# The memory update as one-head products on four column strips

## The chip, the cores and the metric

The kernel runs on one core of a Trainium2 chip. The metric is the device time of one execution in microseconds, the median over runs. Engines are named as in the profile: PE is TensorE (PEld its weight loads), DVE is VectorE, ACT is ScalarE, POOL is GpSimd, SP is SyncE, which issues most transfers.

## The reference

One normalised input goes through a segmented attention with a memory and through a gated unit; both are added to the input. There are 2048 tokens of width 448, 16 heads of 28, and 4 segments of 512 tokens. Cut to what matters here:

```python
phi = lambda t: jnp.where(t > 0, t + 1.0, jnp.exp(t))
for s in range(N):
    qs, ks, vs = q[:, :, s], k[:, :, s], v[:, :, s]
    logits = jnp.einsum("bhqd,bhkd->bhqk", qs, ks) * scale + mask
    p = _softmax(logits, axis=-1)
    a_dot = jnp.einsum("bhqk,bhkd->bhqd", p, vs)
    pq = phi(qs)
    num = jnp.einsum("bhld,bhde->bhle", pq, M)
    den = jnp.einsum("bhld,bhd->bhl", pq, z)[..., None] + 1e-6
    outs.append(g * (num / den) + (1.0 - g) * a_dot)
    pk = phi(ks)
    M = M + jnp.einsum("bhld,bhle->bhde", pk, vs)
    z = z + jnp.einsum("bhld->bhd", pk)
# with xn the layer norm of x:
return x + attention(xn) @ wo + ((sigmoid(xn @ w_gate) * (xn @ w_up)) @ w_down)
```

The change concerns the last two lines of the loop: `M` and `z`, the memory of each head.

## The kernel before, in words

The kernel has two parts. The front goes through the four segments, called blocks, `b` = 0 to 3. For each block it makes the values of four token tiles (`values`, L361), then keys and queries in seven chunks of 128 columns (`keys_queries`, L381), called the seven steps `k` below, and interleaves with them the normalising and transposing of the next block's tokens (`normalise`, `turn`, L103). Behind the front come the attention over keys and values (scores L639, sums L725), the gated unit (L255, L181) and the output product (L824), interleaved by a plan of ticks. TensorE, ScalarE and VectorE run each in the order in which the program issues for them; in the front the order of POOL and SP is left to the framework.

For blocks 0 to 2 the memory is updated in the front. `key_rows` (steps 2 to 5) transposes a chunk of phi of the keys (L401) and copies it to `kn`: tokens on partitions, four token tiles, 448 key columns. `vst` holds the values of the block: tokens on partitions, 16 heads of 32 columns, of which 28 are values and 4 are ones, so that a product with `kn` gives `M` and `z` at once. `update(b, i)` handles group `i` of four heads: four products, one for each token tile, of 112 key columns with 128 value columns. Their 112x128 result holds the wanted 28x32 blocks of the four heads on its diagonal and products of different heads beside it; `heads`, a mask of ones and zeros made once by POOL (L522 to L526), clears these. VectorE multiplies by it and adds the old memory (L412 in block 0, L415 and L416 later). The memory `mst` is two sets of four tiles of 112x128, so packed, that blocks use in turn. Updates of groups 0 and 1 stand in steps 4 and 5, those of groups 2 and 3 in step 6. Their banks of PSUM are "pd" and "m" in turn; there is one bank each.

The memory is read by `recall` (L427): one product of a 112x128 memory tile with phi of the queries (112x512), for group `i`. The recalls of block 1 stand in block 2, those of block 2 at the beginning of block 3, those of block 3 at its end. What they give is weighed and goes to DRAM by a transfer that POOL issues (L431).

In the attention, `Unit.finish` (L725) already uses the four column strips of TensorE's array: head `j` of a group writes partitions `32j` to `32j + 31` of one bank:

```python
for kb in range(NT):
    for j in range(HG):
        T.matmul(pa[32 * j:32 * j + 32, kb * P:], self.vv[:, kb, 32 * j:32 * j + 32],
                 self.pairs[j // 2].block(j % 2, kb), start=kb == 0, stop=kb == NT - 1)
```

Of the kernel before, what the change touches and what calls it, by code (L numbers as in the profile page):

```python
# [9 lines left out]
F32 = mybir.dt.float32  # L10
F32R = mybir.dt.float32r
AF = mybir.ActivationFunctionType
ALU = mybir.AluOpType
# [3 lines left out]
P = 128  # L17
D = 448
H = 16
DH = 28  # L20
# [3 lines left out]
NT = 4  # L24
F = 1792
NF = F // P
HG = 4
NG = H // HG
GW = HG * DH
# [40 lines left out]
def kernel(  # L70
# [10 lines left out]
    nc = tc.nc  # L81
    V, A, G, T = nc.vector, nc.scalar, nc.gpsimd, nc.tensor
# [33 lines left out]
    def x_block(b):  # L116
        return x[b * L:(b + 1) * L, :].rearrange("(t p) d -> p t d", p=P)
# [5 lines left out]
    def bank(name, tag):  # L123
        return ps.tile([P, L], F32, name=name, tag=tag, bufs=banks[tag])
# [5 lines left out]
    def pad(pool, nbytes):  # L130
        pool.tile([P, nbytes // 4], F32, name="pad", tag="pad", bufs=1)
# [3 lines left out]
    def weigh(pool, num, g, add):  # L135

        r = pool.tile([P, 16], F32, name="rc", bufs=2)
        n3 = num.rearrange("p (m c) -> p m c", c=32)
        if add:
            V.tensor_scalar_add(r, n3[:, :, DH], add)  # L140
            V.reciprocal(r, r)
        else:
            V.reciprocal(r, n3[:, :, DH])
        V.scalar_tensor_tensor(n3[:, :, :DH], n3[:, :, :DH], g, r.unsqueeze(2).to_broadcast([P, 16, DH]),
                               op0=ALU.mult, op1=ALU.mult)
# [8 lines left out]
    def eight_k(dtype, name):  # L154
        return mid.tile([P, 8, 256], dtype, name=name, tag="8k")
# [144 lines left out]


    with tc.tile_pool(name="front", bufs=2) as sb, tc.manual_schedule(engines=FRONT):
        heads = sb.tile([P, P], F32, name="heads", bufs=1)
        pad(sb, 192)
        stage = eight_k(F32, "stage").rearrange("p (c a) n -> p c (a n)", c=4)
        vst = eight_k(F32, "vst").rearrange("p (t a) (h c) -> p t (a h) c", t=NT, c=32)
        wv = [late_pair("wv") for _ in range(4)]
        wv = [wv[c // 2][:, c % 2, :] for c in range(8)]
        wqk = [sb.tile([P, 8, P], F32R, name=f"wqk{c}", bufs=1) for c in range(7)]
        mst = [[sb.tile([GW, P], F32, name=f"mst{n}_{i}", bufs=1) for i in range(NG)] for n in range(2)]  # L310
        one = sb.tile([P, 1], F32, name="one", bufs=1)
        kn = eight_k(F32, "kn").rearrange("p (t a) n -> p t (a n)", t=NT)

# [11 lines left out]
        def root(vh):  # L325
            y = sb.tile([P, vh.shape[1]], F32, name=f"y{vh.shape[1]}")
            A.activation(y, vh, AF.Sqrt, scale=-2.0)
            return y
# [40 lines left out]
        def values(b, t):  # L369
            pv = bank("pv", "p")  # L370
            value_terms(b, t, pv, EARLY[1] if b == 0 else TERMS)
            store_values(b, t, pv)
# [29 lines left out]
            n = min(P, D - c * P)  # L402
            A.activation(kn[:, :, c * P:c * P + n], pk.rearrange("p (t n) -> p t n", t=NT)[:, :, :n], AF.Copy)

        def update(b, i):

            pmm = bank("pmm", ("pd", "m")[i % 2])
            for t in range(NT):
                T.matmul(pmm[:GW, :P], kn[:, t, i * GW:(i + 1) * GW], vst[:, t, HG * i:HG * (i + 1), :],  # L409
                         start=t == 0, stop=t == NT - 1)  # L410
            if b == 0:
                V.tensor_mul(mst[1][i], pmm[:GW, :P], heads[:GW])  # L412
            else:
                dm = sb.tile([GW, P], F32, name="dm")
                V.tensor_mul(dm, pmm[:GW, :P], heads[:GW])  # L415
                V.tensor_add(mst[(b + 1) % 2][i], mst[b % 2][i], dm)  # L416

        def phi_queries(b, i):
            phi = sb.tile([GW, L], F32, name="phi", tag="e", bufs=5)
            nc.sync.dma_start(phi, fd[b][i * GW:(i + 1) * GW])  # L420
            return phi

        def recall(b, i, phi):
            ts = sb.tile([P, L], F32, name="ts", bufs=1)
            tb = sb.tile([P, L], F32, name="tb", bufs=2)
            n2 = bank("n2", ("m", "pd")[i % 2])
            T.matmul(n2, mst[b % 2][i], phi, start=True, stop=True)  # L427
            V.transpose(ts, n2)
            weigh(sb, ts, gate[:, i:i + 1], MEM_EPS)
            V.transpose(tb, ts)  # L430
            nc.gpsimd.dma_start(od[b][P * i:P * (i + 1)], tb)  # L431
# [28 lines left out]
        def split_qk(c):  # L460
            r = raw_qk[c].rearrange("p (c n) -> p c n", c=4)
            A.activation(wqk[c][:, 0:4, :], r, AF.Copy)
            G.tensor_sub(wqk[c][:, 4:8, :], r, wqk[c][:, 0:4, :].bitcast(F32))
# [18 lines left out]
        p3, xn, st, y = {}, {}, {}, {}  # L482
# [20 lines left out]
        for t in range(2):  # L503
# [15 lines left out]
        turn_low(3)  # L519
        split_qk(1)  # L520
        split_qk(2)
        G.memset(heads, 1.0)  # L522
        h3 = heads.rearrange("p (j c) -> p j c", c=32)
        G.affine_select(h3, h3, pattern=[[-DH, HG], [0, 32]], base=0, channel_multiplier=1,
                        compare_op=ALU.is_ge, fill=0.0)
        G.affine_select(h3, h3, pattern=[[DH, HG], [0, 32]], base=DH - 1, channel_multiplier=-1,  # L526
                        compare_op=ALU.is_ge, fill=0.0)

        ffn = gated()
        for b in range(NB):  # L530
            last = b == NB - 1
            phi, xn = {}, {}
            if b > 1:
                phi = {i: phi_queries(b - 1, i) for i in range(NG)}
            st = None
            for t in range(3 if b == 0 else 0, NT):
                values(b, t)
                if b > 1 and t > 0:
                    recall(b - 1, t - 1, phi[t - 1])
                if b == 0:  # L540
                    split_qk(t)
                if last:
                    continue
                if t == (3 if b == 0 else 0):
                    mv, vh = statistics(b + 1, 0, NT)
                if t == (3 if b == 0 else 0):
                    st = mv, vh, root(vh)
                if t == (3 if b == 0 else 2):
                    A.activation(one, ident[:, 0:1], AF.Exp)
            if st and b > 0:  # L550
                st = rstd(*st)
                for n in range(2):
                    xn[n] = normalise(b + 1, n, *st[n])
            e = {}
            for k, c in enumerate((3, 4, 5, 6, 0, 1, 2) if last else range(7)):
                e[c] = keys_queries(b, c)
                if b == 0 and c + 4 < 7:
                    split_qk(c + 4)
                if k == 0:
                    if b > 1:  # L560
                        recall(b - 1, NG - 1, phi[NG - 1])
                    if b == 0:
                        st = rstd(*st)
                    if b == 0:
                        A.activation(gate, gate, AF.Exp, scale=-1.0)
                        V.tensor_scalar_add(gate, gate, 1.0)
                        V.reciprocal(gate, gate)
                        V.tensor_scalar(gate_n, gate, -1.0, 1.0, op0=ALU.mult, op1=ALU.add)
                if (b, k) in ((0, 3), (1, 0)):
                    with tc.issue_after(stored[b, c]):  # L570
                        nc.sync.dma_start(acc[b + 2], x_block(b + 2))
                if (b, k) in ((2, 1), (3, 0)):
                    with tc.issue_after(stored[b, c]):
                        next(ffn)
                if last:
                    if k > 0:
                        next(ffn)
                    if 2 <= k < 6:
                        phi[k - 2] = phi_queries(b, k - 2)
                    if k > 4:  # L580
                        begin[k - 5]()
                        recall(b, k - 5, phi[k - 5])
                    continue
                if 2 <= k < 6:
                    key_rows(k - 2, e[k - 2])
                if 4 <= k:
                    update(b, k - 4)
                if k == 6:
                    update(b, 3)
                n = k - 1 if b == 0 else k + 1  # L590
                if 2 <= n < 6:
                    turn(b + 1, n - 2, xn[n - 2])
                if 0 <= n < 4 and n not in xn:
                    xn[n] = normalise(b + 1, n, *st[n])
                if b == 2 and k == 6:
                    next(ffn)
            if last:
                for i in range(2):
                    for _ in range(FILLS[i]):
                        next(ffn)  # L600
                    if i == 0:
                        begin[2]()
                    recall(b, i + 2, phi[i + 2])
# [3 lines left out]
    sb = ctx.enter_context(tc.tile_pool(name="att", bufs=1, reuse_waits="tile"))  # L607
# [234 lines left out]
    with tc.manual_schedule(engines=MANUAL):  # L842
        next(steps)
        k = sum(FILLS) + 6
# [46 lines left out]
```

## Time and profile before

| | |
|---|---|
| median of three runs | 685.7 us (685.55 to 686.2) |
| span of the profiled execution | 684.2 us |
| TensorE busy | 678.0 us (99%) |
| VectorE, ScalarE, POOL busy | 570.1, 338.5, 141.6 us |
| the memory products (L409) | 96 instructions, 34.4 to 115.0 us |
| the recalls (L427) | 24 instructions, 82.6 to 156.4 us |

The span runs from the first to the last instruction of the profiled execution; a time of its own for that execution is not listed, and the runs' times hold 1.5 us (at the median) that the span does not. Busy times are the union of an engine's instructions. A product's recorded duration runs to an estimated end and overlaps the next one's, so prices are read from starts, not from durations. In lines that list a group of instructions, the numbers behind `x` are the busy time of all and the mean of one in ns, and behind the last bar the idle time ahead of them and what ended it. Every f32 product is two instructions on TensorE.

### The profile page before, as it was taken

What the parts mean: (1) busy time and instruction counts of PE and PEld (TensorE: products, weight loads), DVE (VectorE), ACT (ScalarE), POOL (GpSimd) and SP (SyncE); (2) the same over time, 40 slices, a digit from 0 to 9 for tenths busy, and PEclk for the clock granted to TensorE, in tenths of its full rate; (3) what the DMA queues carried; (4) which work ended last, traced back from release to release, by engine and by line L of the source; (5) the groups of instructions that cost most, each with busy time, mean ns of one, the idle gap of its engine ahead of it and who ended that gap; (6) DMA issues with size and microseconds to landing.
All of it is one profiled execution on the core that took longest, in us unless ns stands there. A gap on an engine that the chain in (4) does not pass through costs nothing.

```text
span 684.2 us, 10501 instructions
## 1 busy us (share of the span) xinstructions
PE 678.0 (99%) x3594; PEld 566.7 (83%) x3594; DVE 570.1 (83%) x995; ACT 338.5 (49%) x563; POOL 141.6 (21%) x349
## 2 busy tenths in 40 slices
PE   8999999999999999999999999999999999999998
PEld 7898878778888888888888878788787887888897
DVE  6765696767799899999999899899998999899854
ACT  4836555343365445645456455455554555545320
POOL 3500010101212232232212213133121231221000
PEclk9999999999999999999999999999999999999999
DMA  8446656696223332252424343333353332523352
GB/s 268 173 159 224 214 195 256 234 336 194 71 67 97 104 90 68 57 150 54 108 57 101 91 110 69 100 57 99 84 94 94 97 69 68 115 63 92 86 165 104
DMA packets 45940, 84.37 MB, mean 123 GB/s; under 512 B 6336, under 2 KB 20544, under 8 KB 45376
## 3 DMA queue, kind: packets, MB, share of 16 engines
q1 hardware_dynamic: 42736, 76.26, 37.0%
q0 software_dynamic: 3008, 7.34, 5.2%
q8 instruction: 28, 0.46, 0.3%
q14 instruction: 24, 0.20, 0.1%
q10 hardware_dynamic: 144, 0.11, 0.0%
HBM read 51.05 MB, written 32.64 MB: 122 GB/s over the span
## 4 chain that ended last, share of the span: by engine, by line
PE 97%; DMA 1%; DVE 1%; SPq 0%; ACT 0%; issue 0%; DVEq 0%
PE pgu L255 41%; PE pd L181 20%; PE pp L381 10%; PE st L639 6%; PE pa L725 5%; PE po L824 5%; PE pv L361 5%; PE pmm L409 2%; PE n L427 2%; DMA acc<-in_x 1%; PE pt L103 1%; PE pk L401 1%; DVE stats L320 0%; DVE xs L110 0%; DVE xn L346 0%
## 5 line engine op out<-in xcount | busy, mean ns | idle before, releaser
L255 PE MATMUL pgu<-xs,wgu 128*128 128x512 f32 x1232 | 302.6, 393 | 0.0
L255 PEld LDWEIGHTS pgu<-xs,wgu 128*128 128x128 f32 x1232 | 228.9, 188 | 46.3 <-issue 2.0
L181 PE MATMUL pd<-wdn,hh 128*128 128x448 f32 x672 | 155.3, 366 | 0.0
L181 PEld LDWEIGHTS pd<-wdn,hh 128*128 128x128 f32 x672 | 122.7, 188 | 11.6 <-issue 0.8
L654 POOL TENSOR_SCALAR_AFFINE_SELECT w<-w 128x256 f32<-128x256 f32 (+1 forms) x160 | 76.0, 478 | 231.5 <-ACT w L643 162.4
L707 ACT ACTIVATE w<-w 128x1024 f32<-128x1024 f32 (+1 forms) x96 | 87.8, 915 | 57.6 <-DVE w L703 57.6
L643 ACT ACTIVATE w<-st 128x512 f32<-128x512 f32 x128 | 75.6, 592 | 61.4 <-PE st L639 58.5
L703 DVE TENSOR_TENSOR w<-w,mb 128x1024 f32<-128x1024 f32 (+1 forms) x96 | 100.5, 1054 | 0.8
L661 DVE TRANSPOSE_TENSOR_REDUCE mx<-w 128x32 f32<-128x1024 f32 x64 | 78.9, 1233 | 6.6 <-POOL w L654 6.5
L381 PE MATMUL pp<-xs,wqk 128*128 128x512 f32 x308 | 77.7, 401 | 0.0
L183 DVE TENSOR_TENSOR acc<-pd,acc 128x448 f32<-128x448 f32 x112 | 67.5, 602 | 5.6 <-PE pd L181 5.5
L278 ACT ACTIVATE hh<-sg 128x512 fp32r<-128x512 f32 x56 | 35.4, 631 | 67.9 <-DVE sg L272 46.0
L381 PEld LDWEIGHTS pp<-xs,wqk 128*128 128x128 f32 x308 | 56.8, 188 | 13.4 <-issue 2.4
L639 PE MATMUL st<-qk 84*128 84x128 f32 (+3 forms) x256 | 62.0, 313 | 0.0
L262 ACT ACTIVATE sg<-pgu 128x512 f32<-128x512 f32 x56 | 33.2, 592 | 50.8 <-PE pgu L255 48.9
L639 PEld LDWEIGHTS st<-qk 84*128 84x128 f32 x256 | 47.9, 189 | 8.7 <-issue 1.4
L272 DVE SCALAR_TENSOR_TENSOR sg<-sg,pgu 128x512 f32<-128x512 f32 x56 | 37.7, 673 | 11.2 <-PE pgu L255 11.2
L388 DVE TENSOR_TENSOR qk<-pp,qk 128x512 fp32r<-128x512 f32 x28 | 19.3, 688 | 29.8 <-ACT e L386 23.7
L689 DVE STREAM_TRANSPOSE mb<-top 128x1024 f32<-128x1024 f32 x32 | 39.5, 1235 | 3.3 <-POOL top L686 3.2
L361 PE MATMUL pv<-wv,xs 128*128 128x448 f32 x176 | 39.6, 376 | 0.4 <-DVE xs L110 0.3
L281 DVE SCALAR_TENSOR_TENSOR hh<-sg,hh 128x512 fp32r<-128x512 f32 x56 | 38.1, 680 | 0.9 <-ACT hh L278 0.9
L725 PE MATMUL pa<-w,vv 128*32 128x128 f32 (+3 forms) x512 | 37.8, 436 | 0.0
(100 smaller groups left out, 636.0 us busy)
## 6 DMA issues: line engine op xcount, KB each, us to landing
qk<-qd SPq DMA_DIRECT2D x192, 112.0 KB
qd<-qk SPq DMA_DIRECT2D x28, 512.0 KB
raw<-in_w_ffn SPq DMA_DIRECT2D x14, 512.0 KB
vd<-vst SPq DMA_DIRECT2D x4, 1024.0 KB
vv<-vd SPq DMA_DIRECT2D x16, 256.0 KB
od<-w POOLq DMA_DIRECT2D x16, 256.0 KB, 4.2
sums<-od SPq DMA_DIRECT2D x32, 128.0 KB
out<-acc SPq DMA_DIRECT2D x15, 224.0 KB
```

The source lines that it names most:

```text
L181: T.matmul(pd[:, :D], l, r, start=n == 0, stop=n == len(mms) - 1)
L183: V.tensor_add(acc[b][:, t, :], pd[:, :D], acc[b][:, t, :])
L255: T.matmul(dst, wgu[f][:, w, side * P:(side + 1) * P], xs[b][:, a, :], start=n == 0, stop=n == len(TERMS) - 1)
L361: T.matmul(pv[:, :D], xs[b][:, a, t * P:(t + 1) * P], wv[w], start=n == 0, stop=n == len(TERMS) - 1)
L381: T.matmul(pp, wqk[c][:, w, :], xs[b][:, a, :], start=n == 0, stop=n == len(TERMS) - 1)
L639: T.matmul(st[:, at:at + L - kb * P], self.qk[:KS, 1, h, kb * P:(kb + 1) * P], self.qk[:KS, 0, h, kb * P:], start=True, stop=True)
L643: A.activation(w, st, AF.Copy)
L654: G.affine_select(d, d, pattern=pattern, base=0, channel_multiplier=-1, compare_op=ALU.is_ge, fill=MASK)
L661: V.tensor_reduce(self.mx[:, 32 * h:32 * h + 32], w3[:, h, :2 * L].rearrange("p (b n) -> p b n", n=32), axis=mybir.AxisListType.X, op=ALU. ...
L703: V.tensor_sub(w, w, m)
L707: A.activation(w, w, AF.Exp, scale=SCALE)
L725: T.matmul(pa[32 * j:32 * j + 32, kb * P:], self.vv[:, kb, 32 * j:32 * j + 32], self.pairs[j // 2].block(j % 2, kb), start=kb == 0, stop=k ...
```

## The change

`update` is called once a block, in step 6, and does all four groups in bank "m". Every head has products of its own: 28 key columns with its 32 value columns, for each of four token tiles, head `j` of a group on strip `j`. The results lie dense: head `j` of group `i` on partitions `32j` to `32j + 27`, columns `32i` to `32i + 31`. VectorE copies (block 0) or adds the old sums (later) strip by strip, four instructions, into `dense`, and for each strip a transfer that POOL issues puts the new sums on the packed diagonal of `mst`, whose other parts POOL has set to zero once. The mask is gone, and so is `dm`. `recall` reads a group's slice of the one `mst` tile.

```diff
-        heads = sb.tile([P, P], F32, name="heads", bufs=1)
...
-        mst = [[sb.tile([GW, P], F32, name=f"mst{n}_{i}", bufs=1) for i in range(NG)] for n in range(2)]
+        mst = [sb.tile([GW, NG, HG, 32], F32, name=f"mst{n}", bufs=1) for n in range(2)]
+        dense = [sb.tile([P, NG, 32], F32, name=f"dense{n}", bufs=1) for n in range(2)]
...
-        def update(b, i):
-
-            pmm = bank("pmm", ("pd", "m")[i % 2])
-            for t in range(NT):
-                T.matmul(pmm[:GW, :P], kn[:, t, i * GW:(i + 1) * GW], vst[:, t, HG * i:HG * (i + 1), :],
-                         start=t == 0, stop=t == NT - 1)
-            if b == 0:
-                V.tensor_mul(mst[1][i], pmm[:GW, :P], heads[:GW])
-            else:
-                dm = sb.tile([GW, P], F32, name="dm")
-                V.tensor_mul(dm, pmm[:GW, :P], heads[:GW])
-                V.tensor_add(mst[(b + 1) % 2][i], mst[b % 2][i], dm)
+        def update(b):
+
+            pmm = bank("pmm", "m")
+            for i in range(NG):
+                for t in range(NT):
+                    for j in range(HG):
+                        h = HG * i + j
+                        T.matmul(pmm[32 * j:32 * j + DH, 32 * i:32 * i + 32], kn[:, t, DH * h:DH * (h + 1)],
+                                 vst[:, t, h, :], start=t == 0, stop=t == NT - 1)
+            p3 = pmm[:, :P].rearrange("p (i c) -> p i c", c=32)
+            new, old = dense[(b + 1) % 2], dense[b % 2]
+            for j in range(HG):
+                strip = slice(32 * j, 32 * j + DH)
+                if b == 0:
+                    V.tensor_copy(new[strip], p3[strip])
+                else:
+                    V.tensor_add(new[strip], p3[strip], old[strip])
+                nc.gpsimd.dma_start(mst[(b + 1) % 2][DH * j:DH * (j + 1), :, j, :], new[strip])
...
-            T.matmul(n2, mst[b % 2][i], phi, start=True, stop=True)
+            T.matmul(n2, mst[b % 2][:, i].rearrange("p j c -> p (j c)"), phi, start=True, stop=True)
...
-        G.memset(heads, 1.0)
...
+        for n in range(2):
+            G.memset(mst[n], 0.0)
...
-                if 4 <= k:
-                    update(b, k - 4)
                 if k == 6:
-                    update(b, 3)
+                    update(b)
```

More of the change, by code (lines that the diff above doesn't have):

```diff
@@ L521 @@
         split_qk(2)
-        G.memset(heads, 1.0)
[L523 to L527, printed above, removed]
+        for n in range(2):
+            G.memset(mst[n], 0.0)
         ffn = gated()
```

## The prediction

> **What bounds the kernel now.** I read the page first (the engines' busy times, then the chain that ended last), then the busy time by stretches of the blocks that the change touches, then the line of the memory products.
>
> ```profile
> span 684.2 us, 10501 instructions
> PE 678.0 (99%) x3594; PEld 566.7 (83%) x3594; DVE 570.1 (83%) x995; ACT 338.5 (49%) x563; POOL 141.6 (21%) x349
> PE 97%; DMA 1%; DVE 1%; SPq 0%; ACT 0%; issue 0%; DVEq 0%
> core 0: us, PE busy (x) PEld busy (x) DVE busy (x) ACT busy (x) POOL busy (x), PEclk, DMA share, GB/s
> 20.00:44.60 24.60, 24.60 (x142) 21.21 (x141) 16.48 (x39) 16.15 (x31) 7.88 (x10) 1.00 0.55 209
> 44.60:78.10 33.50, 33.50 (x189) 29.52 (x187) 19.43 (x45) 21.07 (x38) 1.10 (x4) 1.00 0.53 192
> 78.10:115.00 36.90, 36.90 (x196) 30.95 (x195) 29.68 (x68) 20.70 (x38) 3.50 (x8) 1.00 0.61 220
> ```
>
> TensorE carries 97% of the chain. In the three stretches, which end with blocks 0, 1 and 2, it is busy without a gap at a granted clock of 1.00, while VectorE, ScalarE and POOL have room. So a microsecond of TensorE's queue, won or lost here, is a microsecond of the whole.
>
> **The products that go.** First the line, then TensorE's timeline at the end of block 0.
>
> ```profile
> L409 PE MATMUL pmm<-vst,kn x96: 271/273/273, 34.4 to 115.0; 128*112 128x128 f32 x96
> 42.55 1.91 PE L409 MATMUL pmm<-vst,kn 128*112 128x128 f32 x16
> 44.30 0.60 PE L103 MATMUL pt<-ident,xn 128*128 128x128 f32 x4
> ```
>
> Each f32 product is two instructions, so 16 products a block are 32, and 96 in all. The 273 ns of one are not its price, since they overlap: 16 take 44.30 - 42.55 = 1.75 us, 0.109 each. What goes is 32 x 0.109 = 3.49 us a block, 10.5 us in three. By column that is 0.109 / 128 = 0.85 ns.
>
> **The products that come.** A block gets 4 groups x 4 token tiles x 4 heads = 64 products, so 128 instructions with 128 weight loads, each with 28 columns of weights and 32 moving columns. The nearest row is the attention's sum on the same four strips, L725.
>
> ```profile
> 198.92 0.40 PE L639 MATMUL st<-qk 84*128 84x384 f32 x2
> 199.16 1.42 PE L181 MATMUL pd<-wdn,hh 128*128 128x448 f32 x6
> 202.90 0.40 PE L639 MATMUL st<-qk 84*128 84x384 f32 x2
> 203.23 2.36 PE L725 MATMUL pa<-w,vv 128*32 128x512 f32 x32
> 205.52 1.48 PE L181 MATMUL pd<-wdn,hh 128*128 128x448 f32 x6
> 206.83 0.40 PE L639 MATMUL st<-qk 84*128 84x512 f32 x1
> 209.57 1.37 PE L181 MATMUL pd<-wdn,hh 128*128 128x448 f32 x6
> 210.78 0.40 PE L639 MATMUL st<-qk 84*128 84x512 f32 x1
> ```
>
> Its 32 instructions take 205.52 - 203.23 = 2.29 us. They are two passes of 512 + 384 + 256 + 128 columns on each strip, 2560 columns, 2.18 us at 0.85 ns: so the four strips do run at once, with 0.11 to spare. Going in and out costs more: the two L639 ahead take 0.33 (202.90 to 203.23) where the same two take 0.24 (198.92 to 199.16), and the six L181 behind take 1.31 where they take 1.21 elsewhere (209.57 to 210.78). Entry and exit are 0.11 + 0.09 + 0.10 = 0.3 us a block.
>
> At the array's pace the 128 instructions are 32 rounds of 32 columns, 32 x 32 x 0.85 = 0.87 us. But then TensorE must be handed a weight load and a product every 7 ns, and no row shows that for long: L725 averages 2.29 / 32 = 0.072 us. How fast its sequencer hands them over is the disputed cost. These rows bear on it (timelines of the product and weight-load sides, then the sequencer's own instructions by line; L725 starts in three units at 203.23 above and the two starts here).
>
> ```profile
> 11.86 0.47 PE L361 MATMUL pv<-wv,xs 128*128 128x448 f32 x1 [0.29 <-DVE xs L110]
> 11.86 0.30 PEld L361 LDWEIGHTS pv<-wv,xs 128*128 128x128 f32 x2 [0.67 <-DVE xs L110]
> L103 PEldq EVENT_SEMAPHORE  x1: 51/51/51, 13.5 to 13.5; - x1
> 13.55 0.43 PEld L103 LDWEIGHTS pt<-ident,xn 128*128 128x128 f32 x4 [0.18 <-PE pv L361]
> 13.58 0.63 PE L103 MATMUL pt<-ident,xn 128*128 128x128 f32 x4
> L887 PEldq DRAIN  x2: 13/1902/3792, 677.0 to 683.7; - x2
> L824 PE MATMUL po<-wo,xs x19: 360/363/367, 676.8 to 680.4; 128*128 128x448 f32 x19
> 261.53 2.36 PE L725 MATMUL pa<-w,vv 128*32 128x512 f32 x32
> L639 PEldq EVENT_SEMAPHORE  x3: 51/51/51, 262.4 to 262.7; - x3
> 231.79 2.36 PE L725 MATMUL pa<-w,vv 128*32 128x512 f32 x32
> L639 PEldq EVENT_SEMAPHORE  x3: 51/51/51, 233.4 to 233.6; - x3
> L639 PEldq EVENT_SEMAPHORE  x3: 51/51/51, 204.3 to 204.5; - x3
> ```
>
> How far ahead it runs: it reaches the final drain at 677.0, when two of the 19 listed products have started (676.8 and 677.0, 0.2 apart), so it is 17 pairs ahead. How fast: (a) at 11.86, where work had been waiting in line, load and product start together; at 13.5 the line was empty, the sequencer had just waited, and the product comes 0.03 after its load. At 0.03 an entry, a pair is 0.06. (b) The semaphore instruction of the next L639 is reached when all pairs before it are handed over. In the unit of 261.53 those are the 32 of L725, and it is reached 0.9 later; if 17 were ahead at the start, 15 pairs took 0.9, 0.06 a pair. In the unit of 231.79 eleven L255 lie between as well, 43 pairs by 1.6: eleven in 0.7, again 0.06. (c) Against it: in the unit of 203.23 six L181 lie between, 38 pairs by 1.1, six in 0.2, 0.03 a pair. That makes the bounds of the handing over 0.007 (no limit, the array's pace) to 0.06. I take 0.059, by the f32 rows (a) and (b), which are nearest: the same data type, and in (b) the same four strips.
>
> At the update 17 pairs lie ready, and the other 111 come at 0.059: 6.55 us, with entry and exit 6.85. Against 3.49 that is +3.36 a block, **+10.1 us** in three. In this case TensorE stands idle between the small products and nothing fills it, because its queue is in order; behind it VectorE's four sums and the next block's first products come later by as much.
>
> [...]
>
> **The rest of the change, all beside TensorE.**
>
> ```profile
> L415 DVE TENSOR_TENSOR dm<-pmm,heads 112x128 f32<-112x128 f32 x8 | 2.2, 280 | 0.0
> L416 DVE TENSOR_TENSOR mst<-mst,dm 112x128 f32<-112x128 f32 x8 | 2.3, 292 | 0.3
> L412 DVE TENSOR_TENSOR mst<-pmm,heads 112x128 f32<-112x128 f32 x4 | 1.1, 286 | 0.2 <-PE pmm L409 0.2
> L453 POOL MEMSET vst<- 128x256 f32 x1 | 0.3, 306 | 0.0
> L431 POOL DMA_DIRECT2D od<-tb x11 | 6.2, 562 | 81.6 <-DVE tb L430 79.1 <-DVE tm L339 2.5
> 8.61 4.48 POOL L458 TENSOR_TENSOR wv<-wv_raw,wv 128x448 fp32r<-128x448 f32 x4 [6.24 <-ACT wv L457]
> 51.50 0.66 POOL L352 COPY xn<-xn 128x64 f32<-128x64 f32 x2 [13.16 <-DVE xn L346]
> od<-w POOLq DMA_DIRECT2D x16, 256.0 KB, 4.2
> L427 PE MATMUL n<-phi,mst x24: 590/592/594, 82.6 to 156.4; 112*128 112x512 f32 x24
> ```
>
> VectorE loses 2.2 + 2.3 + 1.1 = 5.6 us and gets 12 copies or sums with the same 128 elements a partition, 12 x 0.28 = 3.4 us; zero on the path, as VectorE has 14 us to spare in block 1's stretch. At each block's end four queue up where four (two in block 0) stood, about 1.1 us; behind them are the next block's statistics. The next user of their bank "m" comes in a later block.
>
> POOL loses the mask's three instructions and gets two memsets of 512 elements, about 2 x 0.6 us by L453's row; it sits idle 6.24 us before 8.61, so zero, and without that cover at most 1.2. It issues 12 small transfers of 14 KB, four a block, at 0.56 each by L431's row: 2.2 us behind sums that end some 1.5 us after the products (44.30 in block 0), so from 46 to 48, inside the 13.16 us that POOL is idle before 51.50. If the products last 3.4 longer, the copies at 51.50 move with everything else. Their first reader, L427 in block 2 at 82.6, reads what block 0 stored, some 30 us later, and the later readers come a block or most of one after their store (the stretches above are 33 to 37 us); with a landing of 4.2 the transfers are hidden. Were that cover gone, each block would pay one landing, about 4 us. SP's queue is not touched. Moving products from the fifth and sixth step to the seventh costs nothing: the fourth group's products ran there before and read the last keys, and bank "m" is free since the keys of the fifth step were copied out.
>
> **The rivals.** *The strips win* (faster): the handing over keeps the array's pace, 0.87 + 0.3 = 1.17 us a block, -2.32, -7.0 in three: 685.7 - 7.0 = 678.7 us. For it: (c) shows 0.03 and may itself have waited for room in the queue, and L725 starts without a hitch. Against: (a), and two of three units at 0.06. It decides below 3.19 / 111 = 0.029 a pair; above that the change loses. [...]
>
> *No difference*: pairs at 0.03, as in (c): 111 x 0.03 + 0.3 = 3.63, +0.14 a block, +0.4: 686.1 us. That the strips would not overlap with so few columns ends near by: 128 x 32 x 0.85 = 3.48, and 0.3, +0.9: 686.6.
>
> *The clock falls too*: with TensorE's array idle for most of 7 us, the granted clock drops and the products behind run slow until it is back. The kernel's start shows such a stretch:
>
> ```profile
> L468 PE MATMUL warm<-ident 128*128 128x128 f32 x20 | 4.5, 422 | 1.5 <-POOL ident masks.py:199 1.5
> ```
>
> The 20 take about 0.21 each (4.5 us less the last one's tail) where 0.109 is the price above, 2.1 us lost. Three times that on top is +6.3: 702.1 us. Against it: the products still come every 0.06 us, and the clock is 1.00 throughout the attention.
>
> **How the numbers follow.** The three runs have a median of 685.7, 1.5 above this execution's span of 684.2; I add to the median. Feed-bound 0.60: 685.7 + 10.1 = 695.8, its own range 693 to 698 (0.05 to 0.065 a pair). No difference 0.17: 686.1 to 686.6. Strips win 0.17. Clock 0.06. The range goes from 685.5 to 702.5: it holds all but the win. Faster by over 0.2% (what a measurement here can tell from no change) 0.17, within it 0.17, slower 0.66.
>
> **What would show it.** Each update should take 6.85 us from its first product to the next line's, with products about 0.06 apart after the first 17 pairs; 1.2 would mean the strips win, 3.6 no difference. The granted clock should stay 1.00, L427 should wait for no transfer, and all stretches outside the three updates should keep their lengths. The prediction is wrong if the sequencer hands over f32 pairs much faster than 0.06, so that 0.9 and 1.6 above were waits for room in the queue.

## The result and the profile after

The changed kernel takes 679.53 us at the median (679.4 to 680.37) where the kernel before takes 685.95 in the same runs (685.55 to 687.16): a ratio of 0.9909, 95% interval 0.9895 to 0.9923. That is 6.4 us faster. The forecast was 695.8 us, slower by 10.1; the rival "the strips win" had 678.7.

The page of the kernel after, its first lines and its chain:

```profile
span 677.8 us, 11106 instructions
PE 671.3 (99%) x3882; PEld 558.9 (82%) x3882; DVE 569.2 (84%) x987; ACT 338.6 (50%) x563; POOL 149.3 (22%) x360
PE 97%; DMA 1%; DVE 1%; SPq 0%; ACT 0%; issue 0%; DVEq 0%
```

TensorE has 288 instructions more and 6.7 us less to do, and the chain is its own as before. Its timeline at the ends of the three blocks shows where the time went. First the kernel before, where each block ends with the start of the next block's first value product:

```profile
44.66 0.45 PE L361 MATMUL pv<-wv,xs 128*128 128x448 f32 x1
78.09 0.45 PE L361 MATMUL pv<-wv,xs 128*128 128x448 f32 x1
115.03 0.45 PE L361 MATMUL pv<-wv,xs 128*128 128x448 f32 x1
```

Then the same three places in the kernel after, with the updates ahead of them:

```profile
40.52 1.28 PE L412 MATMUL pmm<-vst,kn 128*28 128x32 f32 x128
41.73 0.66 PE L103 MATMUL pt<-ident,xn 128*128 128x128 f32 x4
42.15 0.45 PE L361 MATMUL pv<-wv,xs 128*128 128x448 f32 x1
72.26 1.28 PE L412 MATMUL pmm<-vst,kn 128*28 128x32 f32 x128
73.47 0.47 PE L361 MATMUL pv<-wv,xs 128*128 128x448 f32 x1
108.32 0.47 PE L361 MATMUL pv<-wv,xs 128*128 128x448 f32 x1
```

Block 1 took 78.09 - 44.66 = 33.43 us and takes 73.47 - 42.15 = 31.32; block 2 took 36.94 and takes 34.85. Both lose 2.1. An update's 128 instructions take 41.73 - 40.52 = 1.21 us; the products that went cost 3.49. The difference is 2.28. About 0.09 of it is lost going in (the last dense product ahead takes 0.32 instead of 0.23 until the next start) and 0.06 going out, which leaves the 2.1. Behind block 2 little changes: 684.2 - 115.03 = 569.2 before, 677.8 - 108.32 = 569.5 after. Block 0 ends 2.5 earlier, 0.4 more than its update explains, and that part is already there at block 0's first key product:

```profile
20.12 7.19 PE L381 MATMUL pp<-xs,wqk 128*128 128x512 f32 x31
19.69 7.69 PE L381 MATMUL pp<-xs,wqk 128*128 128x512 f32 x33
```

The first row is before, the second after. The experiments' profiles have this start between 19.63 and 19.84, one of them with the mask and without strips at 19.84, so it is not tied to the change; what made it 20.12 in that one execution stays open.

Beside TensorE, in the kernel after (VectorE's and POOL's groups, and the transfers):

```profile
L419 DVE COPY dense<-pmm 28x128 f32<-28x128 f32 x4 | 1.1, 285 | 0.1
L421 DVE TENSOR_TENSOR dense<-pmm,dense 28x128 f32<-28x128 f32 x8 | 2.3, 285 | 0.2
L529 POOL MEMSET mst<- 112x512 f32 x2 | 1.0, 524 | 0.0
L422 POOL DMA_DIRECT2D mst<-dense x12 | 7.3, 618 | 28.1 <-DVE dense L421 22.9 <-DVE dense L419 5.2
mst<-dense POOLq DMA_DIRECT2D x12, 14.0 KB, 3.2
```

VectorE's 12 strips take 3.4 us, POOL's two memsets 1.0, its 12 issues 0.62 each, and a transfer lands 3.2 after its issue. No wait of TensorE's on any of these is listed between 20 and 160 us.

### The profile page after: what moved, and what is told of

Read it like the earlier page. It is cut to its first block, busy times and chain, and to the rows that moved or that the text cites. A ratio compares the mean times of both kernels' runs of the same rounds, so it can differ in the third digit from the quotient of the medians.

```text
span 677.8 us, 11106 instructions
## 1 busy us (share of the span) xinstructions
PE 671.3 (99%) x3882; PEld 558.9 (82%) x3882; DVE 569.2 (84%) x987; ACT 338.6 (50%) x563; POOL 149.3 (22%) x360
## 4 chain that ended last, share of the span: by engine, by line
PE 97%; DMA 1%; DVE 1%; SPq 0%; ACT 0%; issue 0%; DVEq 0%
PE pgu L255 42%; PE pd L181 20%; PE pp L381 10%; PE st L639 6%; PE pa L725 5%; PE po L824 5%; PE pv L361 5%; PE n L433 2%; DMA acc<-in_x 1%; PE pt L103 1%; PE pk L401 1%; PE pmm L412 1%; DVE stats L320 0%; DVE xn L346 0%; DVE xs L110 0%
```

## The experiments

**Is it the strips?** Four kernels ran on the same chip, where the kernel before takes 685.6. The first puts before's four-head products together, without strips:

```diff
+            for i in range(NG):
+                for t in range(NT):
+                    T.matmul(pmm[:GW, P * i:P * (i + 1)], kn[:, t, i * GW:(i + 1) * GW],
+                             vst[:, t, HG * i:HG * (i + 1), :], start=t == 0, stop=t == NT - 1)
...
-                if 4 <= k:
-                    update(b, k - 4)
                 if k == 6:
-                    update(b, 3)
+                    update(b)
```

> The kernel before, with its four dense products a group, but all four groups together in step 6 and in one bank; no strips, mask and two VectorE operations a group as before. Theory A (the gain is TensorE time of the products, made by the strips): 32 products a block stay at 0.109 us each, 3.49 us, and the time stays at 685.9 within 0.5. Rival (the gain comes from putting the updates together, or from the bank and the waits that this frees): about 679.5.

685.67 us, ratio 1.0002 (0.9993 to 1.0012). Moving alone is worth nothing.

The second makes the small products on one strip, head by head:

```diff
-                for t in range(NT):
-                    for j in range(HG):
+                for j in range(HG):
+                    for t in range(NT):
...
-                        T.matmul(pmm[32 * j:32 * j + DH, 32 * i:32 * i + 32], kn[:, t, DH * h:DH * (h + 1)],
+                        T.matmul(pmm[:DH, 32 * h:32 * h + 32], kn[:, t, DH * h:DH * (h + 1)],
...
```

> The changed kernel with the same 128 small products a block, but all on one strip (partitions 0 to 27 of the result, 32 columns for each head, the four token tiles of a head in a row). Theory A (four strips at once): on one strip each product waits for the one before, 27 to 29 ns apart, 3.5 to 3.7 us a block instead of 1.1, so 679.5 + 3 x 2.5 = 687.0 (686.5 to 687.5). Rival (a small product costs no more than its handing over, 8.6 ns, wherever it runs): 679.5.

687.49 us, ratio 1.0027 (1.0017 to 1.0037). Theory A holds: small products alone lose 1.9 us.

The third keeps the strips and takes 128 columns:

```diff
-                        T.matmul(pmm[32 * j:32 * j + DH, 32 * i:32 * i + 32], kn[:, t, DH * h:DH * (h + 1)],
-                                 vst[:, t, h, :], start=t == 0, stop=t == NT - 1)
+                        T.matmul(pmm[32 * j:32 * j + DH, P * i:P * (i + 1)], kn[:, t, DH * h:DH * (h + 1)],
+                                 vst[:, t, HG * i:HG * (i + 1), :], start=t == 0, stop=t == NT - 1)
...
```

> The changed kernel on four strips, but each head's keys meet the values of all four heads of the group, 128 moving columns instead of 32; VectorE takes the wanted quarter. Theory A (a round of four costs its moving columns at 0.85 ns): 32 rounds of 0.109 us, 3.49 us a block as before the change, and entry and exit on top: 679.5 + 3 x 2.4 = 686.7 (686.2 to 687.2). Rival (what counts is the small weight loads, or the strips as such): 679.5.

686.84 us, ratio 1.0020 (1.0011 to 1.0030). The strips alone lose too: the gain needs four strips and few columns. In these two kernels VectorE's sums and POOL's transfers are as many as in the kernel after, so the gain does not come from them.

The fourth changes the order of the products:

```diff
-                for t in range(NT):
-                    for j in range(HG):
+                for j in range(HG):
+                    for t in range(NT):
```

> The changed kernel on four strips with 32 columns, the four token tiles of a head in a row and only then the next strip (i, j, t instead of i, t, j). If TensorE takes its line in order, eight instructions of one strip follow each other at 27 to 29 ns and the strips hardly overlap: about 3.5 us a block, 687.0. If its line sorts the strips apart, it stays at 679.5. In between, if it looks ahead by fewer than eight: 681 to 685.

683.18 us, ratio 0.9966 (0.9954 to 0.9978): in between. TensorE's timelines of the four at the end of block 0, in this order:

```profile
40.55 3.66 PE L410 MATMUL pmm<-vst,kn 128*112 128x128 f32 x32
44.05 0.60 PE L103 MATMUL pt<-ident,xn 128*128 128x128 f32 x4
40.60 3.92 PE L412 MATMUL pmm<-vst,kn 128*28 128x32 f32 x128
44.45 0.66 PE L103 MATMUL pt<-ident,xn 128*128 128x128 f32 x4
40.60 3.70 PE L412 MATMUL pmm<-vst,kn 128*28 128x128 f32 x128
44.23 0.66 PE L103 MATMUL pt<-ident,xn 128*128 128x128 f32 x4
40.56 2.55 PE L412 MATMUL pmm<-vst,kn 128*28 128x32 f32 x128
43.05 0.66 PE L103 MATMUL pt<-ident,xn 128*128 128x128 f32 x4
```

From start to next line: 3.50 us for 32 dense products, 3.85 on one strip (0.030 a product), 3.63 with 128 columns (0.113 a round of four), 2.49 by head. Against the 1.21 of the kernel after, three times the difference is 6.9, 7.9, 7.3 and 3.8 us, and the four times lie 6.1, 8.0, 7.3 and 3.7 above 679.5. The first lies 0.8 lower, mostly because it does not pay for going in and out.

**What sets 1.21 us?** Eight columns instead of 32; the sums of the other 24 columns of each head are left out:

```diff
-                        T.matmul(pmm[32 * j:32 * j + DH, 32 * i:32 * i + 32], kn[:, t, DH * h:DH * (h + 1)],
-                                 vst[:, t, h, :], start=t == 0, stop=t == NT - 1)
+                        T.matmul(pmm[32 * j:32 * j + DH, 32 * i:32 * i + 8], kn[:, t, DH * h:DH * (h + 1)],
+                                 vst[:, t, h, :8], start=t == 0, stop=t == NT - 1)
...
```

> The changed kernel with 8 moving columns a product instead of 32; the other 24 columns of each head's sums are left out. It separates the array from the handing over: in the changed kernel a round of four takes 29 ns for the first eight rounds and 33 to 34 ns after. If 33 ns is the pace at which the sequencer hands over (8.4 ns a pair), the late rounds stay at 33 to 34 and an update stays near 1.1 us: 679.3 to 679.6. If both are the array's pace by columns, rounds fall to 10 to 20 ns and an update to 0.6: about 678.

679.79 us, where the kernel before takes 686.0, ratio 0.9908 (0.9893 to 0.9923). Its update:

```profile
40.55 1.24 PE L412 MATMUL pmm<-vst,kn 128*28 128x8 f32 x128
41.72 0.66 PE L103 MATMUL pt<-ident,xn 128*128 128x128 f32 x4
```

1.17 us with a quarter of the columns. From the starts of single instructions, the rounds of four up to the eighth take 28 ns (29 with 32 columns; the very first takes 49), those from the eleventh on 33 to 34 in both. So 32 columns are not the limit. In the first eight rounds products start about 7 ns apart, mostly, and from the eleventh on a pair comes every 8.4 ns: there the weight loads, too, start evenly, 8 to 9 ns apart, in both kernels. That is read here as the pace at which the sequencer hands over when nothing lies ready any more. Of the forecast's terms, this is the one that was 0.059. Whether the 28 ns are four starts of 7, or the least time between two products on one strip (29 in the run on one strip), these runs do not separate.

**How the semaphore rows were misread.** The widths of the attention's sums in another order:

```diff
-            for kb in range(NT):
+            for kb in (0, 3, 2, 1):
...
```

> The changed kernel, with the attention's sums (L725 of before) in the order of widths 512, 128, 256, 384 instead of 512, 384, 256, 128; the same products. It tests how the prediction read the sequencer's semaphore instructions behind them. Where eleven gate products lie between, the semaphore instruction is reached 1.56 us after the first sum. If that is the pace of handing over (43 pairs at 0.06 less those ready), it stays at 1.56. If the sequencer waits for room in TensorE's line, it moves with the start of the fifth round, which now comes at 1.10: to about 1.13. The time stays at 679.5 in both.

679.65 us. The two rows of this kernel, and then those of the kernel after, in the unit with eleven gate products behind:

```profile
225.35 2.36 PE L725 MATMUL pa<-w,vv 128*32 128x512 f32 x32
L639 PEldq EVENT_SEMAPHORE  x3: 51/51/51, 226.5 to 226.7; - x3
225.11 2.36 PE L725 MATMUL pa<-w,vv 128*32 128x512 f32 x32
L639 PEldq EVENT_SEMAPHORE  x3: 51/51/51, 226.7 to 226.9; - x3
```

The semaphore instruction is reached 1.2 us after the first sum instead of 1.6, though the same 43 pairs had to be handed over; it came just behind the start of the fifth round (by single instructions at 1.18 where that round starts at 1.10, and at 1.56 where it starts at 1.53; 1.13 was forecast). So in this unit the time is read as a wait for room, not as a pace. In the unit with six products behind, row (c) of the prediction, the instruction is reached 1.09 us after the first sum in both orders, though the fourth round moves from 1.21 to 0.99: what it waited for there stays open.

**How long does the pace last?** The products four times over:

```diff
-            for i in range(NG):
+            for i in [i for i in range(NG) for _ in range(4)]:
```

> The changed kernel with every group's products made four times over (the last ones stand), 512 instructions a block on the strips instead of 128. It shows the pace that lasts when nothing lies ready. Theory A with a handing over of 8.4 ns a pair: 96 more rounds at 33.5 ns, 3.2 us a block, 679.5 + 9.65 = 689.2. By the prediction's 0.03 a pair it would be 714, by its 0.06 about 747. If the code has to be fetched faster than it comes, somewhere between 690 and 714.

722.05 us: all numbers missed, and only the last clause names what the trace shows. TensorE's timeline in block 1, and its waits in all three updates:

```profile
85.99 2.40 PE L412 MATMUL pmm<-vst,kn 128*28 128x32 f32 x250
91.39 1.80 PE L412 MATMUL pmm<-vst,kn 128*28 128x32 f32 x128 [3.00 <-issue]
95.12 1.93 PE L412 MATMUL pmm<-vst,kn 128*28 128x32 f32 x128 [1.93 <-issue]
99.12 0.32 PE L412 MATMUL pmm<-vst,kn 128*28 128x32 f32 x6 [2.08 <-issue]
PE pmm L412 <- issue: 21.2, 9, 3.4
```

After 250 products TensorE stands still with nothing that the profile shows as the releaser, and then again after every 128: nine gaps, 21.2 us. With their loads, 128 products are 256 instructions. The transfers have a kind "instruction"; in block 0, where the first gap comes after 154 products and ends at 44.67, the stretch from 41 to 42 us holds this and no other transfer:

```profile
q8 instruction: 1, 0.02, 9.2%
```

It is 16 KB, by estimate some 250 instructions at 65 bytes, if the 0.51 MB of the 31 such transfers in the kernel after are divided evenly over its 3882 pairs. The next three follow 3.6 to 4.0 us apart, about as the bursts do. Windows over the three updates show a granted clock of 0.71 to 0.76. That is a mean: in block 0 it is 1.00 up to 47 us and 0.50 from 47.3 to 57.4.

To see whether it is code, 2.5 us of dense products were put between the four times:

```diff
+            for again in range(4):
+                for n, (a, w) in enumerate(TERMS if again else ()):
+                    T.matmul(between, wqk[6][:, w, :], xs[b][:, a, :], start=n == 0, stop=n == len(TERMS) - 1)
+                for i in range(NG):
...
```

> As the kernel that makes every group's products four times over, but the four times in turn over all groups (128 instructions each), and between them eleven dense f32r products of 512 columns into a spare bank, 2.5 us, that nothing reads. With four times in one go, TensorE stood still for 1.8 to 3.6 us after the first 154 to 250 instructions and then after each further 128, and the profile has a 16 KB transfer of instructions at each of these places. If those gaps are code that is not there yet, 2.5 us of dense products between give it the time to come, and the gaps inside the updates go: a block gets three more times 1.1, three times 2.5 and 1.0 for going in and out, 11.8 us, 679.5 + 35.5 = 715. If the gaps come from the number of small products (TensorE's line, or its clock), they stay, some 2.7 us each, nine or more in all: 739 or more.

719.72 us with 99 dense products more; the waits between 40 and 150 us, and the start and the end of the first block's update:

```profile
PE pmm L416 <- issue: 3.2, 3, 2.1
PE between L411 <- issue: 0.3, 1, 0.3
40.53 1.28 PE L416 MATMUL pmm<-vst,kn 128*28 128x32 f32 x128
41.74 2.83 PE L411 MATMUL between<-xs,wqk 128*128 128x512 f32 x11
44.51 1.28 PE L416 MATMUL pmm<-vst,kn 128*28 128x32 f32 x128
49.67 1.21 PE L411 MATMUL between<-xs,wqk 128*128 128x512 f32 x4
51.15 1.88 PE L411 MATMUL between<-xs,wqk 128*128 128x512 f32 x7 [0.27 <-issue]
52.96 1.22 PE L416 MATMUL pmm<-vst,kn 128*28 128x32 f32 x121
54.88 0.26 PE L416 MATMUL pmm<-vst,kn 128*28 128x32 f32 x7 [0.70 <-issue]
```

With the same number of small products TensorE now stands still for 3.5 us instead of 21.2, seven of twelve bursts take the 1.21 of the kernel after, and the clock stays at 1.00. That rules out the number of small products as the cause. That TensorE waits for code is read from where the gaps are. In block 0 the first one falls among the dense products, and the second comes 7 + 121 = 128 pairs later. Counted from the start of TensorE's program, with weight loads, products and semaphore instructions, all thirteen gaps of the two kernels stand at the same place in a block of 256 instructions (192 or 193 past a multiple of 256), and each ends 2.3 to 3.0 us after a 16 KB transfer began. A burst with its dense products is 139 pairs every 3.95 us, a little more than the 128 pairs every 3.7 us that the transfers bring, so some gaps are left. The 715 was missed by these, which cost some 4.5 us by the starts.

**Are the small transfers hidden?** Each was sent twice:

```diff
+                for _ in range(2):
+                    nc.gpsimd.dma_start(mst[(b + 1) % 2][DH * j:DH * (j + 1), :, j, :], new[strip])
```

> The changed kernel with each of the 12 small transfers sent twice. If they are hidden, 679.5 within 0.3. Rival (POOL's issuing, 0.6 us each, or their landing is on the path): eight of them hold POOL for about 5 us a block instead of 2.5, and the next tokens' copies or the recalls come later: up to 2.5 a block, 687.

679.80 us, ratio to before 0.9911 (0.9894 to 0.9927), next to 0.9909. They are hidden.

**A version without them.** The recall reads `dense` in place, on row and column strips:

```diff
+            for i in range(NG):
+                for j in js:
+                    rows = slice(32 * j, 32 * j + DH)
+                    T.matmul(n2[j][32 * i:32 * i + 32], dense[b % 2][rows, i, :], phi[i][rows],
+                             start=True, stop=True)
...
```

> A version meant to be faster than both: the recall reads the dense sums where they lie, so the packed memory, its zeros and the 12 small transfers go. Head j of each group has its rows on partitions 32j on, so a head's product is 28 rows by 32 columns of the array, and two row strips with four heads each run together into two banks; phi of the queries is loaded to the strips by four transfers a group instead of one. TensorE: a block's four recalls of 2 x 0.43 us (3.5 us) become two of 2 x 0.43 with about 0.3 for going in and out, 2.4 us: 679.5 - 3 x 1.1 = 676.2. Rival: different row strips do not run together, or 16 transfers in place of 4 hold the products up: 679.5 to 683.

The second kernel puts all four row strips together:

> As the recall on strips, but all four row strips, 16 heads, at once into four banks (the two of tag s as well). TensorE: 2 x 0.43 and 0.3 a block instead of 3.5, so 679.5 - 3 x 2.3 = 672.5. Rival: the transposes of the next block or the first scores wait for the two banks until VectorE has emptied them (about 2.4 us a bank by the rows of the recall's VectorE operations): up to 3 us a block is given back, 676 to 682.

705.01 and 712.18 us, where the kernel before takes 685.73, ratios 1.0291 (1.0274 to 1.0308) and 1.0386 (1.0366 to 1.0407): both much slower, and beyond their rivals. From the first kernel, TensorE's timeline and the idle time ahead of the recalls:

```profile
89.88 1.09 PE L433 MATMUL n<-phi,dense 28*32 28x512 f32 x16
90.90 0.50 PE L380 MATMUL pp<-xs,wqk 128*128 128x512 f32 x1
  DMA phi<-fd: 13.6, 16
```

Where phi was there, eight heads took 1.02 us, and two row strips do run together: one after the other they would take an estimated twice 0.87, at 0.85 ns a column. But a recall now needs phi of all four groups, in 28-row pieces. Of the 13.6 us of waits for them, weight loads waited 10.7 and products 2.9. The granted clock fell as well, to 0.95 between 75 and 110 us and 0.97 between 110 and 160. How the 25 us over the kernel after divide between these was not worked out. That the order of the old recalls, group by group, had hidden the transfers is argued here, not shown.

## Why the prediction was wrong

The step that failed is the price of handing over in "The products that come": "I take 0.059". It measures 0.0084 a pair, and 0.007 while pairs lie ready, so an update is 1.21 us from its first product to the next line's, where 6.85 was forecast. The bound "0.007 (no limit, the array's pace)" was right to within a fifth, and the rival built on it, "the strips win", was right in sign and nearly in size: 678.7 against 679.5. It had an update with going in and out at 1.17 us, by columns at 0.85 ns; the runs show 1.21 + 0.15 = 1.36, set by starting and handing over and not by columns. Three times the difference is 0.6 of the 0.8 us.

Row by row: (b) was a wait for room and not a pace. The run with another order shows this for its second unit, the one with eleven gate products; in its first unit the instruction is reached at 0.90 in both orders, just behind the third round, which starts at 0.88 in both. That agrees, but the other order does not test it. The prediction named this possibility in its last sentence but gave the forecast built on its own reading a chance of 0.60. It also assumed that TensorE's line holds 17 pairs on the strips as it does for dense products; it holds more, since all 43 pairs were handed over when the fifth round of four started, some 26 ahead. (c), 0.03 a pair, was the better row, still 3.6 times too slow; what set it is open. (a) was one product after one wait, and one start is no pace; why it came 0.03 after its load was not tried. The clock rival did not occur in the kernel after (1.00 in the stretches of all three updates), but the quadruple burst shows a fall: a granted clock of 0.71 to 0.76 in the mean of each update, where TensorE stood idle nine times for 21.2 us in all, 3.4 at the longest. At the kernel's start, which the prediction took for such a stretch, the 20 products stand 0.213 us apart from 1.9 to 5.74 us, but the first record of the granted clock in that trace begins at 5.78 us, at 1.00: the pace is measured there, the clock is not.

Right were the saturated TensorE, by which the gain inside three updates is the gain of the whole, and the zero for VectorE, POOL, the transfers and the move. Of the 0.3 for going in and out, the 0.09 ahead came as forecast, the 0.10 behind was 0.06, and the 0.11 in between cannot be told apart inside the 1.21.

## What to carry to other kernels

Where only the diagonal blocks of a product are wanted, consider making the blocks alone, one on each column strip, with the strips innermost in the loop: a round of four took little more than one such product on one strip (29 to 34 ns against 29), here 1.21 us instead of 3.49, while on one strip or with all columns the same change loses. Bursts of 128 pairs ran without a gap in the kernel after, and in the quadruple run TensorE stood still after 154 to 250 pairs and then after every 128, which is read as code that came at 128 pairs per 3.7 us; dense products between the bursts brought 21.2 us of gaps down to 3.5. And before a time at which a sequencer reaches something is taken for a pace, see whether it moves with the work ahead of it: here 1.56 us became 1.18 when the widths changed their order.

## What was not expected of the hardware

- Load and product pairs come every 8.4 ns when nothing lies ready: rounds of four at 33 to 34 ns with 32 columns (the kernel after) and with 8.
- In the quadruple run TensorE stood still after 154 to 250 pairs at that pace, and then started 128 pairs every 3.7 to 4.0 us: nine gaps, 21.2 us. With the four of the run with dense products between, they stand at one place in every block of 256 instructions.
- On the strips the order of issue counts: by head, with eight instructions of a strip in a row, the update takes 2.49 us, between the 1.21 with the strips innermost and the 3.85 of one strip. Most starts in that run come 4 and 25 ns apart in turn, as if two strips ran at a time. That TensorE looks past some but not all of a strip's waiting work would explain it; no run here shows it.
